# Splitting each K and V load into two column halves issued from two queues, with the slots in memory order

## The chip, the cores and the metric

The kernel runs on one core of one Trainium2 chip. The metric is the device time of one launch in microseconds (us): the kernel before takes 2564.84 us, the median of 3 runs (2564.63 to 2564.92). TensorE is called PE, VectorE DVE, ScalarE ACT, GpSimd POOL and SyncE SP below; a core also has 16 DMA engines, on which every transfer runs.

## What is computed

Two independent attention blocks A and B, each one decode step with a cached K and V, joined at the end:

```python
def _A_ref(x, k_cache, v_cache, wq, wo):
    B, Sq, D = x.shape                 # 8, 1, 1024
    H, Dh = 32, 128
    q = (x @ wq).reshape(B, Sq, H, Dh).transpose(0, 2, 1, 3)
    scores = jnp.einsum("bhqd,bhkd->bhqk", q, k_cache) * (Dh ** -0.5)
    p = softmax(scores)
    o = jnp.einsum("bhqk,bhkd->bhqd", p, v_cache)
    return o.transpose(0, 2, 1, 3).reshape(B, Sq, H * Dh) @ wo
...
return jnp.concatenate([a, b], axis=-1)
```

Everything is bf16. k_cache and v_cache are 8 x 32 x 4096 x 128, that is 268 MB each, and there are four of them; wq and wo are 8.4 MB each. There is one query per batch entry and head, so every byte of K and V is read once and used once.

## The kernel before

**Slots.** The work is cut into 64 slots (NS), 32 for A and 32 for B. A slot n is one batch entry b and one group g of 8 heads. Its K and its V are 8 MB each: 8 heads x 1 MB, which lie next to each other in the cache. `source` (line 292) lays such a block over 128 partitions, 16 partitions to a head, so a partition holds 256 positions of 128 values: one contiguous run of 64 KB. `where` (line 295) gives the order of the slots: b runs fastest, then g, then the block A or B. Consecutive slots are therefore 32 MB apart in the cache.

**Buffers and loads.** kbuf has two buffers of 8 MB (slot n uses n % 2), vbuf one. `load_k` and `load_v` issue one DMA each, all from SP, so all bulk loads stand in one queue in the order of the program. In slot n of the loop (line 497; m = n - 1) the code has load_k(n), then load_v(m), but SP only waits on semaphores and runs ahead of the other engines: as soon as PE has finished the product with V of a slot, vbuf is free, and SP issues the next V and the K two slots on, one behind the other. wq of A and B go through vbuf ahead of the slots. At the end wo of A goes to kbuf buffer 0, the last V (slot 63) to kbuf buffer 1, and wo of B, in five pieces of falling size, again to buffer 0. Pieces of wo are loaded as rows of 64 KB cut in columns: the first piece has runs of 32 KB at a distance of 64 KB.

**One slot of compute.** DVE multiplies K in place by the query, which has been spread over the partitions, in four chunks (`multiply`, L337); PE adds up the 128 values of each position with matmuls against an identity (`add_up`, L347); DVE finishes each chunk (`reduce`, L359) and finds the maximum (`softmax`, L364 to L368). Then PE does the product of slot m's probabilities with V (`pv`, L396), ACT takes the exponentials of slot n (`exps`, L375, eight of them), copies the product out (`copy_o`, L403), and PE gathers it (`gather`, L411) and sums the rows (`rowsum`, L381). Every second slot PE and ACT make the spread query for two slots (`make_qbc`, L325 and L329) from a small copy by POOL (`pick_q`, L318).

**Waits.** A small class Program records what each operation reads and writes by names (k0 and k1 for the two K buffers, v for vbuf) and works out the semaphore waits. PE, ACT and DVE run slots 1 to 62 as a hardware loop of two slots per turn (`rolled`); SP's and POOL's programs are written out. Within a loop nothing but the semaphores' registers changes from turn to turn.

Of the kernel before, what the change touches and what calls it, by code (L numbers as in the profile page):

```python
# [27 lines left out]
class Program:  # L28


    def __init__(self):
        self.order = {e: [] for e in ENGINES}
        self.ops = []
        self.writer = {}
        self.readers = {}
        self.bank = {}
        self.loops = {e: [] for e in ENGINES}

    def add(self, eng, emit, reads=(), writes=(), banks=(), dma=None):
# [104 lines left out]
def _build(nc, caches, out):  # L144
# [23 lines left out]
    with es:  # L168
# [53 lines left out]
        def dma(eng, dst, src, writes, sem, reads=()):  # L222
            return P.add(eng, lambda e: e.dma_start(dst, src), reads=reads, writes=writes, dma=sem)  # L223
# [28 lines left out]
                op.sig = True  # L252

        def load_wq(c):
            dma("sp", vbuf[:], caches[c][3].rearrange("(p r) n -> p (r n)", r=R), ["v"], "v")

        def make_xT(c):
            def emit(e):
# [8 lines left out]
        def make_q(c):  # L267
            w = vbuf[:].rearrange("p (r n) -> p r n", r=R)

            def emit(e):  # L270
                last = None
                for r in range(R):
                    for k in range(8):
                        q = k % 4
                        last = e.matmul(qps[k // 4][0][32 * q:32 * q + B, :], xT[:, c, r, :], w[:, r, k * 512:(k + 1) * 512],  # L275
                                        start=(r == 0), stop=(r == R - 1), tile_position=(0, 32 * q))
                return last
            P.add("pe", emit, reads=["v", "orow"], banks=["oacc", "late"])
            for k in range(2):
                P.add("dve", lambda e, k=k: e.tensor_copy(qrow[k][0], qps[k][0][:]), writes=[qrow[k][1]], banks=[qps[k][1]])  # L280

            def turn(e):
                last = None
                for h in range(H):
                    q, k = (h // 4) % 4, h // 16
                    last = e.matmul(bps[:, h * B:(h + 1) * B], qrow[k][0][:, (h % 4) * Dh:(h % 4 + 1) * Dh],  # L286
                                    ident[:, 32 * q:32 * q + B], start=True, stop=True)
                return last
            P.add("pe", turn, reads=["asb", "osum", "ident"], banks=["bps"])
            P.add("dve", lambda e: e.tensor_copy(qT[:, c, :], bps[:, 0:H * B]), writes=[f"qT{c}"], banks=["bps"])  # L290

        def source(c, what, b, g):
            return caches[c][what][b, g * HP:(g + 1) * HP].rearrange("h (p t) d -> (h p) (t d)", t=T)

        def where(n):
            gi, b = divmod(n, B)
            c, g = divmod(gi, NG)
            return c, g, b

        def load_k(n):  # L300
            c, g, b = where(n)
            dma("sp", kbuf[:, n % 2, :], source(c, 1, b, g), [f"k{n % 2}"], f"k{n % 2}")

        def load_v(m):
            c, g, b = where(m)
            buf, name = (vbuf[:], "v") if m < NS - 1 else (kbuf[:, m % 2, :], f"k{m % 2}")
            dma("sp", buf, source(c, 2, b, g), [name], name)
            vplace[m] = (buf, name)

        def load_wo(c):  # L310
            rows = caches[c][4].rearrange("(p r) n -> p r n", r=RW)
            for j, (lo, hi) in enumerate(pieces[c]):
                dma("sp", wo[:, lo:hi, :], rows[:, lo:hi, :], [f"wo{j}"] if j else ["wo0", "k0"], f"wo{j}")

        def pick_q(n):
            c, g, b = where(n)
            src = qT[:, c, g * HP * B:(g + 1) * HP * B].rearrange("p (h b) -> p b h", b=B)[:, b:b + 2, :]
            P.add("pool", lambda e: e.tensor_copy(qg[:], src.unsqueeze(3).to_broadcast([128, 2, HP, SEG])),  # L318
                  reads=[f"qT{c}"], writes=["qg"])

# [14 lines left out]
        def multiply(n, ch):  # L335
            kv = chunk(n, ch).rearrange("p (t d) -> p t d", d=Dh)
            P.add("dve", lambda e: e.tensor_tensor(  # L337
                kv, kv, qbc[:, n % 2, :].unsqueeze(1).to_broadcast([128, CT, Dh]), ALU.mult),
                reads=[f"k{n % 2}", "qbc"], writes=[f"prod{n % 2}c{ch}"])

        def add_up(n, ch):
            i = ch % 2
            pj = chunk(n, ch).rearrange("p (t j w) -> p t j w", t=CT, w=EW)
            rv = red[i][:].rearrange("p (t w) -> p t w", w=EW)

            def emit(e):
                first = e.matmul(rv, ident[:], pj[:, :, 0, :], start=True, stop=False).ins  # L347
# [6 lines left out]
            P.add("pe", emit, reads=[f"prod{n % 2}c{ch}", f"k{n % 2}", "ident"], banks=[f"red{i}"])  # L354

        def reduce(n, ch):
            i = ch % 2
# [31 lines left out]
        def pv(m):  # L389
            buf, name = vplace[m]  # L390

            def emit(e):
                last = None
                for j in range(CT):
                    q, t = j % 4, j * TB
                    last = e.matmul(oacc[32 * q:32 * q + TB * HP, 0:TB * Dh],  # L396
                                    prob[:, t:t + TB, :].rearrange("p t h -> p (t h)"), buf[:, t * Dh:(t + TB) * Dh],
                                    start=(j < 4), stop=(j >= CT - 4), tile_position=(0, 32 * q))
                return last
            P.add("pe", emit, reads=[name] + probs, banks=["oacc"])  # L400

        def copy_o(m):
            P.add("act", lambda e: e.activation(osb[:], oacc[:], ACTF.Copy), writes=scores, banks=["oacc"])  # L403
# [11 lines left out]
        def heads(m):  # L415
            i = m % 2
            o = 32 + i * HP
            gi, b = divmod(m % NS, B)
# [4 lines left out]
            P.add("dve", lambda e: e.tensor_tensor(on[:, i, :], sps[:, o:o + HP], rl[:, i, :], ALU.mult),  # L423
                  reads=[f"rl{i}"], writes=[f"on{i}"], banks=["sps"])
            P.add("pool", lambda e: e.tensor_copy(ona[:, gi, :, b], on[:, i, :]), reads=[f"on{i}"], writes=[f"ona{gi}"])  # L425
# [28 lines left out]
        def project(c, j):  # L454
            lo, hi = pieces[c][j]

            def emit(e):
                last = None
                for r in range(lo, hi):
                    for q in range(4):  # L460
                        last = e.matmul(acc[32 * q:32 * q + B, 0:CW], onp[:, r, :], wo[:, r, q * CW:(q + 1) * CW],  # L461
                                        start=(r == 0), stop=(r == RW - 1), tile_position=(0, 32 * q))
                return last
            P.add("pe", emit, reads=["onp", f"wo{j}", "k0"], banks=["acc"])

        def write_out(c):
            P.add("dve", lambda e: e.tensor_copy(orow[0:104, :], acc[0:104, 0:CW]), writes=["orow"], banks=["acc"])
# [12 lines left out]
            P.add("pe", emit, reads=["ident"], banks=["red0"])  # L480

        NS = NC * NG * B
        vplace = {}
        pieces = [[(0, RW)], [(0, 16), (16, 24), (24, 28), (28, 30), (30, RW)]]
        load_wq(0)
        load_k(0)
# [9 lines left out]

        for n in range(NS):
            m = n - 1
            if n == NS - 1:
                for e, at in marks().items():  # L500
                    P.loops[e].append((start[e], at, (n - 1) // 2))
            if n == 1:
                start = marks()
            if n >= 1:
                load_k(n)
            if n == NS - 1:
# [33 lines left out]
                pv(m)  # L540
            if n % 2 == 1 and n + 1 < NS:
                make_qbc(n + 1)
            exps(n)
            if m >= 0:
                copy_o(m)
# [43 lines left out]
        def rolled(name, eng, a, b, k):  # L589
            ahead, base, waits = P.rolled(name, a, b, k)  # L590
            for key, val in ahead.items():
                eng.wait_ge(sems[key], val)
            regs = {}
            for key, val in base.items():
                regs[key] = eng.alloc_register(f"w{a}_{key}")
                eng.reg_mov(regs[key], val)
            with eng.Fori(0, k):
                for op, ws in zip(P.order[name][a:], waits):
                    for key, inc in ws:
                        eng.wait_ge(sems[key], regs[key])  # L600
                        eng.reg_add(regs[key], regs[key], inc)  # L601
                    one(name, eng, op)

        def run(name, eng):
            ops, at = P.order[name], 0
# [62 lines left out]
```

## Time and profile before

| | |
|---|---|
| median of 3 runs | 2564.84 us (2564.63 to 2564.92) |
| span of the profiled execution, first to last instruction | 2563.2 us |
| time of the median run that lies around that span | 1.6 us |
| read from HBM | 1107.33 MB, 432 GB/s over the span |
| DVE busy | 1360.0 us, 53% of the span |
| PE busy | 1470.8 us, 57% |
| ACT busy | 652.1 us, 25% |
| mean granted TensorE clock | 0.798 |

The profiled execution's own time is taken as its span and the 1.6 us around it. A row of the timeline gives start, duration, engine, line, operation, written tile <- read tile, the count, and in brackets the idle time ahead of it with what ended it. "SPq" and "ACTq" are the DMA issues of SP and ACT. A row of DMA queues gives packets, MB, and the time that the packets took, as a share of the time of 16 engines in the stretch asked for; a packet counts to the stretch in which it starts, with its whole time, so the share can be over 100%. q1 is SP's queue, q10 ACT's; q8 and q14 fetch instructions.

### The profile page before, as it was taken

Reading aid. Unit: us, or ns where it says so; the run is one execution under the profiler, and the core shown is the slowest. Engines: PE = TensorE matmul, PEld = TensorE weight load, DVE = VectorE, ACT = ScalarE, POOL = GpSimd, SP = SyncE. Lnnn points to the kernel's source line nnn. Section 1 sums busy time; section 2 is a strip of 40 time slices with the busy share of each in tenths; the row PEclk is TensorE's granted clock in tenths of the full one; section 3 lists DMA queues with packets and bytes.
Section 4 is the critical chain, followed back from the end, with each engine's and each line's share of the span. In section 5 each row is a group of like instructions: output and inputs, shape, how many; then the busy total and the mean of one; then the engine's idle time right before and its main releaser. Section 6 shows DMA issues by size and latency. Waiting matters only on the chain.

```text
span 2563.2 us, 19013 instructions
## 1 busy us (share of the span) xinstructions
PE 1470.8 (57%) x9440; PEld 291.3 (11%) x5600; DVE 1360.0 (53%) x913; ACT 652.1 (25%) x1127; POOL 291.1 (11%) x112
## 2 busy tenths in 40 slices
PE   3565565565565565565565565555655655655656
PEld 0101101101101101101011011011011011011012
DVE  3456455455465465465464564564564564554551
ACT  0322322312312313313313313213223223223122
POOL 0111011011011011011011011011011010110110
PEclk8787787787787887887887887877877877878878
DMA  9999999999999999999999999999999999999999
GB/s 425 428 438 430 438 430 437 430 437 431 436 432 436 432 436 432 435 433 435 432 436 432 436 432 436 431 437 431 437 431 437 430 438 430 438 430 438 430 437 386
DMA packets 19755, 1107.52 MB, mean 432 GB/s; under 512 B 2256, under 2 KB 2320, under 8 KB 2592
## 3 DMA queue, kind: packets, MB, share of 16 engines
q1 hardware_dynamic: 19616, 1107.31, 99.9%
q8 instruction: 7, 0.11, 0.0%
q10 hardware_dynamic: 128, 0.06, 0.0%
q14 instruction: 4, 0.03, 0.0%
HBM read 1107.33 MB, written 0.03 MB: 432 GB/s over the span
## 4 chain that ended last, share of the span: by engine, by line
DMA 63%; PE 17%; DVE 14%; issue 6%; SPq 0%; another core or an unknown queue 0%; DVEq 0%
DMA kbuf<-in_B_k_cache_dram 31%; DMA kbuf<-in_A_k_cache_dram 30%; PE red L347 12%; DVE kbuf L337 12%; PE oacc L396 4%; DMA kbuf<-in_B_wo_dram 2%; DVE osb L359 2%; SPq L223 0%; DVE on L423 0%; PE acc L461 0%; DVEq L601 0%; PE oacc L275 0%; PE late L275 0%; PE bps L286 0%
## 5 line engine op out<-in xcount | busy, mean ns | idle before, releaser
L337 DVE TENSOR_TENSOR kbuf<-kbuf,qbc 128x8192 bf16<-128x8192 bf16 x256 | 1128.2, 4408 | 782.9 <-DMA kbuf<-in_A_k_cache_dram 389.8
L347 PE MATMUL red<-kbuf,ident 128*128 128x512 bf16 x4096 | 1050.9, 419 | 392.9 <-DVE kbuf L337 218.7
L375 ACT ACTIVATE prob<-osb,bias 128x256 bf16<-128x256 f32 x512 | 598.7, 1583 | 930.4 <-PE oacc L396 895.6
L425 POOL COPY ona<-on 128x8 bf16<-128x8 bf16 x64 | 278.7, 4354 | 2218.2 <-DVE on L423 2218.2
L411 PE MATMUL sps<-sel,osb 128*128 128x8 f32 x512 | 116.6, 357 | 649.9 <-ACT osb L403 649.7
L359 DVE TENSOR_REDUCE osb<-red 128x64 f32<-128x512 f32 x256 | 176.0, 687 | 305.9 <-PE red L347 305.9
L375 ACT ACTIVATION_READ_ACCUMULATOR prob<-osb,bias 128x1 f32 x512 | 252.9, 494 | 0.0
L329 ACT ACTIVATE qbc<-bps 128x256 bf16<-128x256 f32 x32 | 12.3, 383 | 897.6 <-PE bps L325 897.6
L396 PE MATMUL oacc<-vbuf,prob 128*32 128x512 bf16 x4032 | 231.8, 383 | 10.5 <-DMA vbuf<-in_B_v_cache_dram 10.5
L411 PEld LDWEIGHTS sps<-sel,osb 128*128 128x128 f32 x512 | 112.4, 323 | 669.7 <-issue 667.8
L347 PEld LDWEIGHTS red<-kbuf,ident 128*128 128x128 bf16 x256 | 25.1, 98 | 1191.0 <-issue 1170.3
L396 PEld LDWEIGHTS oacc<-vbuf,prob 128*32 128x32 bf16 x4032 | 102.5, 97 | 324.6 <-issue 219.1
L403 ACT ACTIVATE osb<-oacc 128x512 f32<-128x512 f32 x64 | 38.2, 597 | 15.3 <-PE oacc L396 8.2
L381 PE MATMUL sps<-rsum,ones 128*128 128x8 f32 x128 | 36.6, 360 | 5.4 <-ACT prob L375 5.4
L381 PEld LDWEIGHTS sps<-rsum,ones 128*128 128x128 f32 x128 | 34.7, 331 | 5.5 <-ACT prob L375 5.5
L364 DVE TENSOR_REDUCE rmax<-osb 128x1 f32<-128x256 f32 x64 | 26.9, 420 | 7.6
L423 DVE TENSOR_TENSOR on<-sps,rl 128x8 bf16<-128x8 f32 x64 | 10.1, 158 | 27.9 <-PE sps L381 27.9
L365 DVE STREAM_TRANSPOSE tmax<-rmax 128x32 f32<-128x32 f32 x64 | 13.5, 212 | 7.7
L366 DVE TENSOR_REDUCE nmax<-tmax 128x2 f32<-128x32 f32 x64 | 11.9, 186 | 7.6
L318 POOL COPY qg<-qT 128x256 bf16<-128x256 bf16 x32 | 12.5, 392 | 28.0 <-DVE qT L290 27.4
L368 DVE SCALAR_TENSOR_TENSOR bias<-nmax,neg 128x8 f32<-128x8 f32 x64 | 10.7, 168 | 7.7
L275 PE MATMUL oacc<-vbuf,orow 128*8 128x512 bf16 x64 | 7.7, 472 | 11.4 <-DMA vbuf<-in_A_wq_dram 11.4
(52 smaller groups left out, 104.1 us busy)
## 6 DMA issues: line engine op xcount, KB each, us to landing
kbuf<-in_B_wo_dram SPq DMA_DIRECT2D x1, 4096.0 KB, 39.5
kbuf<-in_B_wo_dram SPq DMA_DIRECT2D x1, 2048.0 KB, 44.0
kbuf<-in_B_wo_dram SPq DMA_DIRECT2D x1, 1024.0 KB, 46.1
kbuf<-in_B_wo_dram SPq DMA_DIRECT2D x2, 512.0 KB, 47.2
kbuf<-in_A_k_cache_dram SPq DMA_DIRECT2D x32, 49.1
vbuf<-in_A_v_cache_dram SPq DMA_DIRECT2D x32, 30.2
kbuf<-in_B_k_cache_dram SPq DMA_DIRECT2D x32, 49.1
vbuf<-in_B_v_cache_dram SPq DMA_DIRECT2D x31, 30.1
```

Of the source, the lines that this page charges most:

```text
L318: P.add("pool", lambda e: e.tensor_copy(qg[:], src.unsqueeze(3).to_broadcast([128, 2, HP, SEG])), reads=[f"qT{c}"], writes=["qg"])
L337: P.add("dve", lambda e: e.tensor_tensor(kv, kv, qbc[:, n % 2, :].unsqueeze(1).to_broadcast([128, CT, Dh]), ALU.mult), reads=[f"k{n % 2}", ...
L347: first = e.matmul(rv, ident[:], pj[:, :, 0, :], start=True, stop=False).ins
L359: P.add("dve", lambda e: e.tensor_reduce(score[:, ch * CT:(ch + 1) * CT], rv, AX.X, ALU.add), writes=[f"score{ch}"], banks=[f"red{i}"])
L364: P.add("dve", lambda e: e.tensor_reduce(rmax[:], score, AX.X, ALU.max), reads=scores, writes=["rmax"])
L365: P.add("dve", lambda e: e.transpose(tmax[:], rmax[:].to_broadcast([128, 32])), reads=["rmax"], writes=["tmax"])
L375: P.add("act", lambda e, h=h: e.activation(prob[:, :, h], score, ACTF.Exp, bias=bias[:, h:h + 1], scale=scale, accum_out=rsum[:, i, h:h + 1]),
L381: P.add("pe", lambda e: e.matmul(sps[:, i * HP:(i + 1) * HP], ones[:].to_broadcast([128, 128]), rsum[:, i, :], start=True, stop=True), rea ...
L396: last = e.matmul(oacc[32 * q:32 * q + TB * HP, 0:TB * Dh], prob[:, t:t + TB, :].rearrange("p t h -> p (t h)"), buf[:, t * Dh:(t + TB) * D ...
L403: P.add("act", lambda e: e.activation(osb[:], oacc[:], ACTF.Copy), writes=scores, banks=["oacc"])
L411: last = e.matmul(sps[:, o:o + HP], osb[:, t * Dh:(t + 1) * Dh], sel[:, t, :], start=(t == 0), stop=(t == TB - 1))
L425: P.add("pool", lambda e: e.tensor_copy(ona[:, gi, :, b], on[:, i, :]), reads=[f"on{i}"], writes=[f"ona{gi}"])
```

## The change

Each K and each V load of a slot becomes two loads. The left one takes the first 32 KB of every partition's 64 KB run, the right one the other 32 KB. The left ones stay on SP; the right ones go to ACT, in `load_right(n)`, which stands behind make_qbc and ahead of exps: there ACT issues the right half of V of slot n and of K of slot n + 2. The first two K and the first V are issued by SP in both halves, and the last V (slot 63) stays one load on SP. The right halves have names and semaphores of their own (k0r, k1r, vr): multiply and add_up of chunks 0 and 1 wait for the left half only, chunks 2 and 3 for the right one; pv waits for both halves of V.

Slots now run through g first and then b, which is the order in which their 8 MB blocks lie in the caches. With that the source of a load in ACT's loop is the loop's counter times two plus a constant. As source A ends and B begins inside the slots, ACT has two loops now, with slots written out between and around them; PE and DVE keep their one loop. pick_q takes two neighbouring groups of heads of one batch entry, where it took two neighbouring batch entries of one group.

```diff
         def where(n):
-            gi, b = divmod(n, B)
-            c, g = divmod(gi, NG)
+            c, r = divmod(n, NG * B)
+            b, g = divmod(r, NG)
             return c, g, b
 
-        def load_k(n):
-            c, g, b = where(n)
-            dma("sp", kbuf[:, n % 2, :], source(c, 1, b, g), [f"k{n % 2}"], f"k{n % 2}")
...
+        def load(n, what, buf, name, right, eng=None):
+            c, r = divmod(n, NG * B)
+            if right is None:
+                P.add("sp", lambda e: e.dma_start(buf, source(c, what, r)), writes=[name, name + "r"], dma=name)
+                return
+            cut = slice(T * Dh // 2, T * Dh) if right else slice(0, T * Dh // 2)
+
+            def emit(e):
+                at = r if P.turn is None else P.turn * 2 + r
+                return e.dma_start(buf[:, cut], source(c, what, at)[:, cut])
+            key = name + "r" if right else name
+            P.add(eng or ("act" if right else "sp"), emit, writes=[key], dma=key)
+
+        def load_k(n, right=False):
+            load(n, 1, kbuf[:, n % 2, :], f"k{n % 2}", right, "sp" if n < 2 else None)
+            if n < 2 and not right:
+                load_k(n, True)
...
+        def load_right(n):
+            if 1 <= n < NS - 1:
+                load_v(n, True)
+            if n + 2 < NS:
+                load_k(n + 2, True)
...
-                reads=[f"k{n % 2}", "qbc"], writes=[f"prod{n % 2}c{ch}"])
+                reads=[f"k{n % 2}" + ("r" if ch >= NCH // 2 else ""), "qbc"], writes=[f"prod{n % 2}c{ch}"])
...
-            P.add("pe", emit, reads=[name] + probs, banks=["oacc"])
+            P.add("pe", emit, reads=[name, name + "r"] + probs, banks=["oacc"])
...
             if n % 2 == 1 and n + 1 < NS:
                 make_qbc(n + 1)
+            load_right(n)
             exps(n)
```

SP, at the start of the program (wq of A, K of slot 0, wq of B, K of slot 1, V of slot 0, K of slot 2, V of slot 1, K of slot 3); before:

```order
L223 DMA vbuf<-in_A_wq_dram 128x32768
L223 DMA kbuf<-in_A_k_cache_dram 128x32768
L223 DMA vbuf<-in_B_wq_dram 128x32768 [waits c_pe,d_v]
L223 DMA kbuf<-in_A_k_cache_dram 128x32768
L223 DMA vbuf<-in_A_v_cache_dram 128x32768 [waits c_pe,d_v]
L223 DMA kbuf<-in_A_k_cache_dram 128x32768
```

and with the change, where x2 is a left and a right half one behind the other:

```order
L224 DMA vbuf<-in_A_wq_dram 128x32768
L310 DMA kbuf<-in_A_k_cache_dram 128x16384 x2
L224 DMA vbuf<-in_B_wq_dram 128x32768 [waits c_pe,d_v]
L310 DMA kbuf<-in_A_k_cache_dram 128x16384 x2
L310 DMA vbuf<-in_A_v_cache_dram 128x16384 [waits c_pe,d_v]
L310 DMA vbuf<-in_A_v_cache_dram 128x16384
L310 DMA kbuf<-in_A_k_cache_dram 128x16384
L310 DMA vbuf<-in_A_v_cache_dram 128x16384 [waits c_pe,d_v]
```

From the K of slot 2 on, SP issues left halves alone, with the waits that it had.

ACT, in its loop, one slot with the spread query and one without; before:

```order
L329 ACTIVATE qbc<-bps 128x256
L601 REGISTER_ALU [waits c_dve]
L375 ACTIVATE prob,rsum<-osb,bias 128x256 x8
L601 REGISTER_ALU [waits c_act]
L403 ACTIVATE osb<-oacc 128x512
L601 REGISTER_ALU [waits c_dve]
L601 REGISTER_ALU [waits c_pe]
```

and with the change (d_vr is the semaphore of the right halves of V; the ISA rows set an address):

```order
L351 ACTIVATE qbc<-bps 128x256
L310 ISA
L310 DMA vbuf<-in_A_v_cache_dram 128x16384
L310 ISA
L310 DMA kbuf<-in_A_k_cache_dram 128x16384
L632 REGISTER_ALU [waits c_dve]
L397 ACTIVATE prob,rsum<-osb,bias 128x256 x8
L632 REGISTER_ALU [waits c_act]
L425 ACTIVATE osb<-oacc 128x512
L632 REGISTER_ALU [waits c_pe]
L632 ISA [waits d_vr]
L310 DMA vbuf<-in_A_v_cache_dram 128x16384
```

The two issues stand ahead of the eight exponentials of each slot, behind the same wait for PE's product with V that held the exponentials before.

DVE, in its loop, between chunk 0 and chunk 3 of a slot; with the change there is one more wait (d_k1r, the right half of K) ahead of chunk 2:

```order
L359 TENSOR_TENSOR kbuf<-kbuf,qbc 128x8192
L632 REGISTER_ALU [waits c_pe]
L381 TENSOR_REDUCE osb<-red 128x64
L632 REGISTER_ALU [waits d_k1r]
L359 TENSOR_TENSOR kbuf<-kbuf,qbc 128x8192
L632 REGISTER_ALU [waits c_pe]
L381 TENSOR_REDUCE osb<-red 128x64
```

Ahead of chunk 0 DVE waits for d_k1 as before, which now stands for the left half.

More of the change, by code (lines that the diff above doesn't have):

```diff
@@ L36, in __init__ @@
         self.bank = {}
+        self.turn = None
         self.loops = {e: [] for e in ENGINES}
@@ L254, in load_wq @@
         def load_wq(c):
-            dma("sp", vbuf[:], caches[c][3].rearrange("(p r) n -> p (r n)", r=R), ["v"], "v")
+            dma("sp", vbuf[:], caches[c][3].rearrange("(p r) n -> p (r n)", r=R), ["v", "vr"], "v")
         def make_xT(c):
@@ L277, in emit @@
                 return last
-            P.add("pe", emit, reads=["v", "orow"], banks=["oacc", "late"])
+            P.add("pe", emit, reads=["v", "vr", "orow"], banks=["oacc", "late"])
             for k in range(2):
@@ L290, in make_q, with source, load_v @@
             P.add("dve", lambda e: e.tensor_copy(qT[:, c, :], bps[:, 0:H * B]), writes=[f"qT{c}"], banks=["bps"])
-        def source(c, what, b, g):
-            return caches[c][what][b, g * HP:(g + 1) * HP].rearrange("h (p t) d -> (h p) (t d)", t=T)
+        def source(c, what, r):
+            return caches[c][what].rearrange("b (g h) (p t) d -> (b g) (h p) (t d)", h=HP, t=T)[r]
         def where(n):
-            gi, b = divmod(n, B)
-            c, g = divmod(gi, NG)
+            c, r = divmod(n, NG * B)
+            b, g = divmod(r, NG)
             return c, g, b
-        def load_k(n):
-            c, g, b = where(n)
-            dma("sp", kbuf[:, n % 2, :], source(c, 1, b, g), [f"k{n % 2}"], f"k{n % 2}")
-        def load_v(m):
-            c, g, b = where(m)
+        def load(n, what, buf, name, right, eng=None):
[13 more added lines that the diff above has]
+                load_k(n, True)
+        def load_v(m, right=False):
             buf, name = (vbuf[:], "v") if m < NS - 1 else (kbuf[:, m % 2, :], f"k{m % 2}")
-            dma("sp", buf, source(c, 2, b, g), [name], name)
+            load(m, 2, buf, name, None if m == NS - 1 else right, None if m else "sp")
+            if m == 0 and not right:
+                load_v(m, True)
             vplace[m] = (buf, name)
+        def load_right(n):
[3 more added lines that the diff above has]
+                load_k(n + 2, True)
         def load_wo(c):
@@ L312, in load_wo @@
             for j, (lo, hi) in enumerate(pieces[c]):
-                dma("sp", wo[:, lo:hi, :], rows[:, lo:hi, :], [f"wo{j}"] if j else ["wo0", "k0"], f"wo{j}")
+                dma("sp", wo[:, lo:hi, :], rows[:, lo:hi, :], [f"wo{j}"] if j else ["wo0", "k0", "k0r"], f"wo{j}")
         def pick_q(n):
             c, g, b = where(n)
-            src = qT[:, c, g * HP * B:(g + 1) * HP * B].rearrange("p (h b) -> p b h", b=B)[:, b:b + 2, :]
+            src = qT[:, c, g * HP * B:(g + 2) * HP * B].rearrange("p (i h b) -> p i h b", i=2, b=B)[:, :, :, b]
             P.add("pool", lambda e: e.tensor_copy(qg[:], src.unsqueeze(3).to_broadcast([128, 2, HP, SEG])),
@@ L353, in emit @@
                 return last
-            P.add("pe", emit, reads=[f"prod{n % 2}c{ch}", f"k{n % 2}", "ident"], banks=[f"red{i}"])
+            P.add("pe", emit, reads=[f"prod{n % 2}c{ch}", f"k{n % 2}" + ("r" if ch >= NCH // 2 else ""), "ident"], banks=[f"red{i}"])
         def reduce(n, ch):
@@ L417, in heads @@
             o = 32 + i * HP
-            gi, b = divmod(m % NS, B)
+            c, g, b = where(m % NS)
+            gi = c * NG + g
             if m == NS - 1:
@@ L463, in emit @@
                 return last
-            P.add("pe", emit, reads=["onp", f"wo{j}", "k0"], banks=["acc"])
+            P.add("pe", emit, reads=["onp", f"wo{j}", "k0", "k0r"], banks=["acc"])
         def write_out(c):
@@ L482, in _build @@
         NS = NC * NG * B
-        vplace = {}
+        NH = NG * B
+        vplace, start = {}, {}
         pieces = [[(0, RW)], [(0, 16), (16, 24), (24, 28), (28, 30), (30, RW)]]
@@ L498, in _build @@
             m = n - 1
[L499 to L503, printed above, removed]
+            if n in (1, NH - 3, NH + 1, NS - 3, NS - 1):
+                now = marks()
+                for e, at in now.items():
+                    if n == NH - 3 or n == NS - 3:
+                        if e == "act":
+                            P.loops[e].append((start[e], at, (n - first) // 2))
+                    elif n == NS - 1 and e != "act":
+                        P.loops[e].append((start[e], at, (n - 1) // 2))
+                    if n == 1 or n == NH + 1 and e == "act":
+                        start[e] = at
+                first = n
             if n >= 1:
@@ L596, in rolled @@
                 eng.reg_mov(regs[key], val)
-            with eng.Fori(0, k):
+            with eng.Fori(0, k) as P.turn:
                 for op, ws in zip(P.order[name][a:], waits):
@@ L602, in rolled @@
                     one(name, eng, op)
+            P.turn = None
         def run(name, eng):
```

## The prediction

> **What bounds the kernel now.** I read the page's slices and DMA lines first, then the chain, then the groups with their idle time, then the timeline of one slot. In the page, the DMA row says how busy the 16 engines are in each 40th of the span:
>
> ```profile
> span 2563.2 us, 19013 instructions
> DMA  9999999999999999999999999999999999999999
> DMA packets 19755, 1107.52 MB, mean 432 GB/s; under 512 B 2256, under 2 KB 2320, under 8 KB 2592
> q1 hardware_dynamic: 19616, 1107.31, 99.9%
> DMA 63%; PE 17%; DVE 14%; issue 6%; SPq 0%; another core or an unknown queue 0%; DVEq 0%
> L337 DVE TENSOR_TENSOR kbuf<-kbuf,qbc 128x8192 bf16<-128x8192 bf16 x256 | 1128.2, 4408 | 782.9 <-DMA kbuf<-in_A_k_cache_dram 389.8
> ```
>
> There is no slice in which the DMA engines rest; q1, SP's queue, has them busy for 99.9% of the span. The chain names PE and DVE for a third, but that is only who released SP's issues; DVE's largest group stands idle for 782.9 us, waiting for K. What counts is whether the queue ever runs dry, and one slot of the timeline answers it:
>
> ```profile
> 1011.25 4.43 DVE L337 TENSOR_TENSOR kbuf<-kbuf,qbc 128x8192 bf16<-128x8192 bf16 x1 [12.94 <-DMA kbuf<-in_A_k_cache_dram]
> ...
> 1035.77 3.63 PE L396 MATMUL oacc<-vbuf,prob 128*32 128x512 bf16 x64
> ...
> 1039.50 0.33 SPq L223 DMA_DIRECT2D vbuf<-in_A_v_cache_dram  x1
> 1039.87 0.43 SPq L223 DMA_DIRECT2D kbuf<-in_A_k_cache_dram  x1
> ...
> 1049.95 4.43 DVE L337 TENSOR_TENSOR kbuf<-kbuf,qbc 128x8192 bf16<-128x8192 bf16 x1 [11.82 <-DMA kbuf<-in_A_k_cache_dram]
> ```
>
> K lands at 1011.25, the slot's compute ends 28.25 us later, SP issues the next two loads at 1039.50, and the K in flight then still needs 10.45 us. So about 10.5 us of transfers are left in the queue at each issue: the kernel is bound by what the engines take per packet, and compute has 10.5 us of slack in each slot.
>
> **The change, part by part.** *The shorter runs.* A load of 8 MB is 128 rows of 64 KB, 8 on each engine. Now each row is two packets. What a packet takes is read from stretches that hold one kind: first 200 to 2400 us, then two stretches within the first piece of B's wo (2539.65 to 2546.80 and 2540.5 to 2546.5), whose rows are 32 KB runs at a distance of 64 KB, the very shape of the new halves.
>
> ```profile
> DMA packets 16365, 953.90 MB, mean 434 GB/s; under 512 B 1808, under 2 KB 1808, under 8 KB 1808
> q1 hardware_dynamic: 16363, 953.88, 100.2%
> ...
> q1 hardware_dynamic: 94, 3.08, 100.0%
> ...
> q1 hardware_dynamic: 79, 2.59, 100.2%
> ```
>
> 953.88 MB / 65,536 B is 14,555 packets of 64 KB; 100.2% of 16 x 2200 us is 35,270 us; less the 1808 small ones (9 ns each, below) that is 2422.1 ns per packet. A packet of 32 KB takes 16 x 7150 x 1.000 / 94 = 1217.0 and 16 x 6000 x 1.002 / 79 = 1217.7, so 1217.4 ns. The share over 100% shows that each record overlaps the next: 70 us over 16,363 records, 4.3 ns each. One packet of 64 KB thus costs 2417.8 ns of engine time, two of 32 KB 2 x 1213.1 = 2426.2: **8.4 ns more**, a gap that each packet brings along. Shares are rounded to 0.1%, which leaves about 1.7 ns either way: 6.7 to 10.1 ns.
>
> 64 loads of K and 63 of V are split: 127 x 8 = 1016 more packets on each engine, 1016 x 8.4 ns = **8.5 us** (6.8 to 10.3).
>
> *The second semaphore.* Each load ends with a 4-byte packet on each engine; one of them, alone in 10 ns from 640.825 us:
>
> ```profile
> q1 hardware_dynamic: 1, 0.00, 5.6%
> ```
>
> 5.6% of 160 ns is 9 ns, less the overlap 4.7; 127 more per engine are **0.6 us**.
>
> *Two queues on the same engines.* The only place where SP's and ACT's queues carry data together is the start, where x lies in rows of 2 KB in ACT's queue between SP's 64 KB packets (7.23 to 7.70 us):
>
> ```profile
> q1 hardware_dynamic: 14, 0.92, 450.3%
> q10 hardware_dynamic: 8, 0.02, 8.9%
> ```
>
> A q10 packet takes 83.7 ns there, and the q1 packets of the stretch 4.503 x 7520 / 14 = 2418.8 ns, so no longer than elsewhere: changing queues costs nothing visible, and it hides nothing either, since the second 32 KB of a long packet take 2422.1 - 1217.4 = 1204.7 ns, by which rate 2 KB are 75.3 ns, and 83.7 less the overlap leaves a gap of 4.1 ns. I take 0 for it, from this row. The bounds below are the rivals.
>
> The Trainium skill says in "DMA: Bandwidth & Descriptors", "Issuing engines are not separate DMA queues", that DMAs started by different engines run on the same 16 engines and interleave, and that starting them on several saves only the issue time. By that the sum has no term for the second queue, which agrees with these rows; its being small depends on eight packets.
>
> *ACT's two issues per slot.* They stand ahead of the exponentials. Its issues at the start took 0.59 and 0.29 us, so I estimate 0.6 to 1.2 us per slot.
>
> ```profile
> 0.74 0.59 ACTq L223 DMA_DIRECT2D prob<-in_A_x_dram  x1
> 1.37 0.29 ACTq L223 DMA_DIRECT2D prob<-in_B_x_dram  x1
> ...
> 1049.48 0.60 ACT L403 ACTIVATE osb<-oacc 128x512 f32<-128x512 f32 x1
> ...
> 1051.90 0.57 PE L381 MATMUL sps<-rsum,ones 128*128 128x8 f32 x2
> 1054.51 9.09 PE L347 MATMUL red<-kbuf,ident 128*128 128x512 bf16 x32 [2.03 <-DVE on L423]
> ```
>
> Behind the issues wait exps, the copy (L403), gather and rowsum, and behind these PE's first add_up (L347). PE stands idle there for 2.03 us, which covers them; were it not so, the slack in the queue does. 0 us.
>
> *The order in the two queues.* If the engines take packets from both queues in turn, a slot's right halves pass what SP has queued. At the start before:
>
> ```profile
> 43.61 8.76 DVE L337 TENSOR_TENSOR kbuf<-kbuf,qbc 128x8192 bf16<-128x8192 bf16 x2 [11.93 <-DMA kbuf<-in_A_k_cache_dram]
> ...
> 70.84 0.33 SPq L223 DMA_DIRECT2D vbuf<-in_A_v_cache_dram  x1
> ...
> 82.40 4.43 DVE L337 TENSOR_TENSOR kbuf<-kbuf,qbc 128x8192 bf16<-128x8192 bf16 x1 [8.83 <-DMA kbuf<-in_A_k_cache_dram]
> ```
>
> A load of 8 MB is 19.4 us (8 x 2.42), a half 9.7. Slot 0 starts on its left half 9.7 us earlier, at about 34, and frees its buffer near 57 (four chunks took 24.5 us above, from 1011.25 to 1035.77; two remain when the right half lands at 43.6). ACT then puts K of slot 2, right half, into an empty queue; it shares the engines with wq of B until 69 and with K of slot 1, whose left half lands at 82.4 as now, its right half at 92, V of slot 0 at 111.5, K of slot 2 at 121.2. PE's product with V waits for that V, ends near 115.1, and the next loads are issued at about 115.3 with 5.9 us left in SP's queue, none in ACT's. From there: with M us left in SP's queue at an issue, served at half speed, K lands 2M later; compute takes 28 us more; the engines have 38.7 us of new work. So M becomes 38.7 + M - 2M - 28 = 10.7 - M: 5.9, 4.8, 5.9 and so on. The queues never run dry; half of the slack is gone, at no cost. The 9.7 us gained at the start buy nothing, as the engines were already busy.
>
> *Memory order.* Each load still reads one block of 8 MB in rows of 64 KB distance; only the distance between blocks shrinks. Nothing in the rows depends on it: 0.
>
> *The end.* The last packet of wo is used at 2559.66 (row below), and all ends 3.5 us later; the change moves nothing there. At the last issue of V halves 38.8 + M us of work are queued (wo of A 19.4, two halves of V); K of slot 63 lands after 2M and frees the buffer for the last V 24.5 us on, at 36 for M = 5.9, 8 us before the engines could rest. More of ACT's program is written out, which may add one or two instruction fetches of 16 KB; one such packet at 34.39 us took 6.100 x 160 = 976 ns on one engine, so 0 to 3 us; I take 0, as it delays one engine of 16.
>
> ```profile
> q8 instruction: 1, 0.02, 610.0%
> ...
> 2559.66 0.39 PE L461 MATMUL acc<-kbuf,onp 128*8 128x256 bf16 x8 [0.81 <-DMA kbuf<-in_B_wo_dram]
> ```
>
> **Sum:** 8.5 + 0.6 = 9.1 us on the span of 2563.2, so 2572.3; with the 1.6 us around it, as for the median of 2564.84, **2573.9 us**, 0.35% slower. Its own range is 6.8 + 0.6 to 10.3 + 0.6 + 3: 2572 to 2579.
>
> **The rivals.** *(a) The second queue hides the gap.* While one queue's packet ends, the other's might already flow. If no gap is left, each 32 KB costs the 1204.7 ns by which the longer packet exceeds the shorter one: 1016 x (2417.8 - 2 x 1204.7) = -8.5 us, with the semaphores -7.9, **2556.9 us**, faster. It pays from the point where the gap per packet is under half of 8.4 ns, 4.2, since there are twice as many. For it: nothing yet ran with both queues full. Against it: the 2 KB packets between SP's kept a gap. *(b) Half the gap.* That same 4.1 ns behind a change of queue may hold for long packets too: then the doubled count is paid and only the semaphores are left, **2565.4 us**, no change. The Trainium skill, in "DMA: Bandwidth & Descriptors", "Why small descriptors are slow (HBM only)", gives a fixed overhead of about 3 cycles per packet; with the 850 MHz of "Where 436 GB/s comes from" that is, as an estimate, 3.5 ns and a sum of 3.6 + 0.6 us, inside this case too; the 8.4 ns speak against it. *(c) Changing queues stalls the engine.* Behind an instruction packet of another queue one SP packet took 17.338 x 160 = 2774 ns (the row of 10 ns at 639.36 us):
>
> ```profile
> q1 hardware_dynamic: 1, 0.07, 1733.8%
> ```
>
> That is 352 ns more than 2422. At 2032 changes it is 715 us, 3280 us. The q10 row speaks against it: behind eight changes there was nothing. *(d) The queues run dry,* since ACT's issues or the late half of V cost more than 10.7 us in two slots. Each us beyond it is paid in each of 31 pairs: 2 us beyond give 62 us, 2627.
>
> **How the numbers follow.** 0.2% (5.1 us) is about what a measurement of this kernel tells from no change. Forecast 0.55; (a) 0.18, faster; (b) 0.20, the same; (c) and (d) 0.07 together, slower. So faster 0.18, same 0.20, slower 0.62. The range takes in the forecast, (b), and (a) to its end, and leaves out (c), (d) and a gap somewhat larger than any row shows: 2556.5 to 2580.
>
> **What would show it.** In the new profile: q1 and q10 share the bytes about evenly, some 32,500 packets of 32 KB; right halves of V land about 19 us after their issue and left ones about 30; the time of 16 engines divided by the packets of a stretch gives 1213 ns per 32 KB (1204.7 for (a), 1209 for (b)); DVE still waits for K in each slot, with half of the slack. I am wrong if the DMA row has slices below 9 (d), or if that quotient is not 1213.

## The result and the profile after

The changed kernel takes **2576.32 us** (median of 4 runs, 2575.96 to 2577.2) against 2564.84 us before (2564.63 to 2564.92): 11.5 us more, a ratio of 1.0045 with the interval [1.0033, 1.0057]. The profiled run took 2576.45 us, 2573.9 of them in its span, which is 10.7 us longer than the span before.

The page of the changed kernel: span, the 16 DMA engines in 40 slices, packets, the two queues (packets, MB, share), the chain, and DVE's largest group (busy, mean ns, idle and what ended it).

```profile
span 2573.9 us, 19455 instructions
...
DMA  9999999999999999999999999999999999999998
...
DMA packets 38045, 1107.54 MB, mean 430 GB/s; under 512 B 4288, under 2 KB 4352, under 8 KB 4624
...
q1 hardware_dynamic: 20048, 587.22, 53.0%
q10 hardware_dynamic: 17984, 520.16, 47.0%
...
DMA 55%; PE 19%; DVE 15%; issue 6%; another core or an unknown queue 3%; ACT 2%; SPq 0%; DVEq 0%; ACTq 0%
...
L359 DVE TENSOR_TENSOR kbuf<-kbuf,qbc 128x8192 bf16<-128x8192 bf16 x256 | 1128.3, 4408 | 770.4 <-DMA kbuf<-in_B_k_cache_dram 373.8
```

The bytes are the same, the packets nearly twice as many (38,045 for 19,755), and the engines are still busy in every slice but the last: nothing waits that did not wait before. The same engines simply take longer for the same bytes. How much per packet is read from the stretch of 200 to 2400 us, as for the kernel before:

```profile
DMA  9999999999999999999999999999999999999999
...
DMA packets 32606, 949.89 MB, mean 432 GB/s; under 512 B 3616, under 2 KB 3616, under 8 KB 3616
...
q10 hardware_dynamic: 16301, 474.91, 50.2%
q1 hardware_dynamic: 16302, 474.95, 50.2%
```

The two queues share the bytes evenly. 100.4% of 16 x 2200 us is 35,341 us; less the 3616 small packets at 9 ns, divided by the other 28,987 packets, it is 1218.1 ns per 32 KB. The 0.4% (141 us) over 32,603 records is an overlap of 4.3 ns each, so a packet takes 1213.8 ns net, where 1213.1 was forecast and (a) would have shown 1204.7, (b) 1209.

The timeline of one slot in the middle of the changed kernel (start, duration, what ran, idle time before it in brackets):

```profile
1004.46 0.33 SPq L310 DMA_DIRECT2D vbuf<-in_A_v_cache_dram  x1
1004.74 0.37 ACTq L310 DMA_DIRECT2D vbuf<-in_A_v_cache_dram  x1
1004.83 0.43 SPq L310 DMA_DIRECT2D kbuf<-in_A_k_cache_dram  x1
...
1005.28 0.34 ACTq L310 DMA_DIRECT2D kbuf<-in_A_k_cache_dram  x1
...
1014.94 4.43 DVE L359 TENSOR_TENSOR kbuf<-kbuf,qbc 128x8192 bf16<-128x8192 bf16 x1 [11.85 <-DMA kbuf<-in_A_k_cache_dram]
1015.23 0.60 ACT L425 ACTIVATE osb<-oacc 128x512 f32<-128x512 f32 x1
...
1019.50 9.13 PE L369 MATMUL red<-kbuf,ident 128*128 128x512 bf16 x32 [1.27 <-DVE on L446]
...
1042.66 0.33 SPq L310 DMA_DIRECT2D vbuf<-in_A_v_cache_dram  x1
```

At the issue at 1004.46 the K in flight still needs 10.48 us, as much as before (10.45): the slack of compute has not shrunk. ACT's two issues take 0.37 and 0.34 us, and PE's rest ahead of add_up, which was to cover them, is 1.27 us, down from 2.03.

### The profile page after: what moved, and what is told of

Same layout as the page of the kernel before. It is cut to its first block, busy times and chain, and to the rows that moved or that the text cites. A ratio compares the mean times of both kernels' runs of the same rounds, so it can differ in the third digit from the quotient of the medians.

```text
span 2573.9 us, 19455 instructions
## 1 busy us (share of the span) xinstructions
PE 1480.3 (58%) x9440; PEld 293.3 (11%) x5600; DVE 1360.6 (53%) x913; ACT 655.9 (25%) x1127; POOL 291.2 (11%) x112
## 2 busy tenths in 40 slices
DMA packets 38045, 1107.54 MB, mean 430 GB/s; under 512 B 4288, under 2 KB 4352, under 8 KB 4624
## 4 chain that ended last, share of the span: by engine, by line
DMA 55%; PE 19%; DVE 15%; issue 6%; another core or an unknown queue 3%; ACT 2%; SPq 0%; DVEq 0%; ACTq 0%
DMA kbuf<-in_B_k_cache_dram 29%; DMA kbuf<-in_A_k_cache_dram 19%; DVE kbuf L359 13%; PE red L369 13%; PE oacc L418 5%; DMA kbuf<-in_A_wo_dram 2%; DMA vbuf<-in_A_v_cache_dram 2%; DMA kbuf<-in_B_wo_dram 2%; ACT prob L397 1%; DMA vbuf<-in_B_wq_dram 1%; DVE osb L381 1%; DMA vbuf<-in_A_wq_dram 1%; SPq L310 0%; PE sps L433 0%
## 5 line engine op out<-in xcount | busy, mean ns | idle before, releaser
L484 PE MATMUL acc<-kbuf,onp 128*8 128x256 bf16 x256 | 11.9, 357 | 6.1 <-DMA kbuf<-in_A_wo_dram 4.7
## 6 DMA issues: line engine op xcount, KB each, us to landing
vbuf<-in_A_v_cache_dram SPq DMA_DIRECT2D x33, 4096.0 KB, 30.3
vbuf<-in_A_v_cache_dram ACTq DMA_DIRECT2D x31, 4096.0 KB, 31.1
vbuf<-in_B_v_cache_dram ACTq DMA_DIRECT2D x31, 4096.0 KB, 31.1
```

## The experiments

Runs 1 to 4 were on one chip, runs 5 to 8 on another; the kernel before, run beside them, took 2564.91 us on the first and 2565.0 us on the second. My theory: each packet brings a gap of some 9 ns, whatever queue it comes from, and the 1016 more packets per engine are the loss. The rivals: the second queue costs it (both queues on one engine, ACT's issues, or the queues running dry), or the order of the slots in memory does.

**1. Both halves from SP.** The changed kernel without the second queue:

```diff
-        def load_k(n, right=False):
-            load(n, 1, kbuf[:, n % 2, :], f"k{n % 2}", right, "sp" if n < 2 else None)
...
+        def load_k(n):
+            for right in (False, True):
+                load(n, 1, kbuf[:, n % 2, :], f"k{n % 2}", right, "sp")
...
-            load_right(n)
```

> Both halves of every load are issued by SP, so runs of 32 KB, twice the semaphores and the memory order stay, and the second queue goes. Theory of the gap (each packet costs about 9 ns beside its bytes, whichever queue it is in): 1016 more packets and 127 more semaphore packets per engine, 9.9 us over the kernel before, about 2575 us. Rival, the second queue or ACT's issues cost the time: back to about 2565 us. If the queue costs only what the gap leaves open of the 11.5 us measured, 1 to 2 us under the changed kernel.

Measured: 2574.30 us (2574.14 to 2574.49), ratio 1.0036 [1.0023, 1.005], 9.4 us more than before. From 200 to 2400 us its one queue stands so:

```profile
q1 hardware_dynamic: 32604, 949.89, 100.3%
```

The gap theory holds: of the 11.5 us, 9.4 are there without a second queue. Less 0.6 us for the semaphores (their records take 1.27 us per engine before and 2.41 us here, and 4.3 ns of each of the 127 new ones is overlap) it is 8.8 us, **8.7 ns per added packet**. The rest, 2.0 us here and 1.3 by run 6, comes with the second queue.

**2. Whole loads, two queues.** V(n) and K(n + 2) of odd n are issued by ACT, those of even n by SP, in runs of 64 KB:

```diff
...
+        def load_k(n):
+            if n < 3 or n % 2 == 0:
+                load(n, 1, kbuf[:, n % 2, :], f"k{n % 2}")
...
         def load_right(n):
-            if 1 <= n < NS - 1:
-                load_v(n, True)
-            if n + 2 < NS:
-                load_k(n + 2, True)
+            if n % 2 == 1 and n < NS - 1:
+                load(n, 2, vbuf[:], "v", "act")
+                load(n + 2, 1, kbuf[:, 1, :], "k1", "act")
```

> Loads are whole again (runs of 64 KB, one semaphore each), in memory order, but V of each odd slot and the K two slots on are issued by ACT, those of even slots by SP, so both queues carry data at once for most of the time. Theory of the gap: as many packets as before, about 2565 us, at most 1 us more. Rival, two queues on the same engines cost the time: about 2575 us.

Measured: 2573.52 us, but spread from 2566.7 to 2575.57; ratio 1.0034 [1.0021, 1.0048]. Both theories missed: neither the gap nor a fixed price of a second queue gives 9 us that come and go. The profile is of the run with 2566.7 us. Its packets took no longer (200 to 2400 us: 100.2% for 14,545 packets of 64 KB and 1811 small ones, 2424 ns each, against 2422 before):

```profile
q10 hardware_dynamic: 8289, 483.46, 50.8%
q1 hardware_dynamic: 8067, 469.77, 49.4%
```

but what is left in the queues at an issue swings from slot to slot. Its timeline, a narrow slot and then two neighbours:

```profile
853.79 0.33 SPq L305 DMA_DIRECT2D vbuf<-in_A_v_cache_dram  x1
...
856.74 4.42 DVE L350 TENSOR_TENSOR kbuf<-kbuf,qbc 128x8192 bf16<-128x8192 bf16 x1 [4.32 <-DMA kbuf<-in_A_k_cache_dram]
...
1007.85 0.33 SPq L305 DMA_DIRECT2D vbuf<-in_A_v_cache_dram  x1
...
1011.73 4.43 DVE L350 TENSOR_TENSOR kbuf<-kbuf,qbc 128x8192 bf16<-128x8192 bf16 x1 [5.25 <-DMA kbuf<-in_A_k_cache_dram]
...
1043.14 0.34 ACTq L305 DMA_DIRECT2D vbuf<-in_A_v_cache_dram  x1
...
1055.27 4.43 DVE L350 TENSOR_TENSOR kbuf<-kbuf,qbc 128x8192 bf16<-128x8192 bf16 x1 [13.89 <-DMA kbuf<-in_A_k_cache_dram]
```

K comes 3.9 us after the issue of the next loads, then 12.1, and at 853.79 only 3.0. That is a swing as I had forecast it for the changed kernel, but not with the numbers of that formula: 3.9 and 12.1 add up to 16, where M and 10.7 - M make 10.7, and the next two slots have 8.5 and 12.4. So a new theory for this run: where the swing goes to its narrow side, the queues run dry in some executions. Run 8 tries it.

The trace shows one more thing that can narrow a slot. The issue of a K, 0.43 us in the kernel before, takes 2.2 to 5.2 us in 43 slots of this run, on either engine. Where it is ACT's, the exponentials stand behind it. This is the slot ahead of the narrow one at 853.79:

```profile
813.53 4.12 ACTq L305 DMA_DIRECT2D kbuf<-in_A_k_cache_dram  x1
817.77 1.43 ACT L388 ACTIVATE prob<-osb,bias 128x256 bf16<-128x256 f32 x1 [4.52 <-issue]
```

Each of the eight slots with 4.0 us or less follows such an issue by ACT, of 4 to 5 us. Why the issues take so long is open.

**3. The memory order alone.** The kernel before, with its loads whole and on SP, and only the order of the slots changed:

```diff
-            gi, b = divmod(n, B)
-            c, g = divmod(gi, NG)
+            c, r = divmod(n, NG * B)
+            b, g = divmod(r, NG)
...
```

> The kernel before with only the order of the slots changed (groups of heads first, then batch entries). Theory of the gap: no change, 2565 us within 1 us. Rival, the order in the caches matters for the reads: a time off 2565 by several us to either side; if the order gave a gain that the shorter runs hide, under 2563 us.

Measured: 2564.84 us (2564.66 to 2565.55, 11 runs), ratio 1.0 [0.9991, 1.0009]. The order costs and gains nothing that this shows (the interval is 0.1% to either side, some 2.3 us); as the cause of the 11.5 us it falls.

**4 and 5. Shorter runs still.** Left and right take turns within a row, by 16 KB (two packets of each per row) and by 4 KB (eight of each):

```diff
-            cut = slice(T * Dh // 2, T * Dh) if right else slice(0, T * Dh // 2)
+            def cut(t):
+                return t.rearrange("p (a s w) -> p a s w", s=2, w=T * Dh // 4)[:, :, 1 if right else 0, :]
```

(w=2048 in the second; multiply and add_up wait for the halves accordingly.)

> As the changed kernel, with as many loads, semaphores and queues, but the left load takes quarters 0 and 2 of each row and the right one quarters 1 and 3: runs of 16 KB, 2032 more packets per engine than the changed kernel. Theory of the gap: 2032 x 9.1 ns = 18.5 us more than the changed kernel's 2576.3, about 2595 us. Rival, the loss hangs on the number of loads, the semaphores or the second queue: no change from 2576 us.

Measured: 2593.60 us (2593.52 to 2594.09), ratio 1.0112 [1.0097, 1.0128]. That is 17.3 us over the changed kernel for 127 x 16 = 2032 more packets per engine, **8.5 ns each**. The slices show that the time is no rest; from 200 to 2400 us:

```profile
DMA  9999999999999999999999999999999999999999
...
DMA packets 61120, 942.63 MB, mean 428 GB/s; under 512 B 3586, under 2 KB 3586, under 8 KB 3586
...
q1 hardware_dynamic: 30557, 471.26, 50.3%
q10 hardware_dynamic: 30560, 471.34, 50.3%
```

> As the changed kernel, with as many loads, semaphores and queues, but left and right loads take every other 4 KB of each row: 16 packets where the changed kernel has 2, 14,224 more per engine. Theory of the gap, if each packet of 4 KB brings the 9.1 ns of a longer one: 129 us more, about 2706 us. If the gap of a short packet is the one that the last pieces of wo show (160.4 ns less 4.3 of overlap less 150.6 at the full rate: 5.5 ns): 16 x 156.1 - 2 x 1213.6 = 70 ns per 64 KB, 72 us more, about 2648 us. Rival, the loss hangs on loads, semaphores or queues: about 2576 us.

Measured: 2724.91 us (2722.41 to 2725.4, one at 2759.11), ratio 1.0664 [1.0607, 1.0722]: 131.3 us over run 4 for 127 x 96 = 12,192 more packets per engine, 10.8 ns each. The expectation with 9.1 ns was 19 us short, that with 5.5 ns 77. The engines do not rest here either, in the same stretch:

```profile
DMA  9999999999999999999999999999999999999999
...
DMA packets 223401, 901.05 MB, mean 410 GB/s; under 512 B 3424, under 2 KB 3424, under 8 KB 223398
```

But the 10.8 ns are not all gap. By the MB of the three stretches (949.86, 942.60 and 901.02 in 16 x 2200 us), 64 KB take an engine 2428.6 ns in the changed kernel, 2447.3 in run 4 and 2560.3 here: 18.7 ns for 2 more packets and 113.0 ns for 12 more, **9.4 ns each** both times. At that price the 12,192 packets make 114.6 us; the other 17 us are paid outside the stretch. Near the end the engines rest for some 7 us; from 2660 to 2680 us, in slices of 0.5 us:

```profile
DMA  9999999999999999977642100000000000990000
```

At the start SP's issues take long, and the packets with them: 183.8 ns each from 70 to 120 us, 164.0 from 200 to 2400, which is some 5 us per engine. Where the last 4 or 5 us go is not traced.

```profile
72.97 21.95 SPq L311 DMA_DIRECT2D vbuf<-in_A_v_cache_dram  x2
```

So the gap comes with every added packet, 8.7 to 9.4 ns, from 64 KB down to 4 KB. What no run parts is the packet from the jump: each added packet also starts a run that does not adjoin the one before it.

**6. The changed kernel again,** unchanged, beside the runs that follow.

> The changed kernel as it is, so that it stands on the same chip as the run with all halves on ACT. 2576 us if the 2.0 us by which it exceeded the run with both halves on SP belong to it; about 2574.5 us if they were the chip's.

Measured: 2575.58 us (2574.67 to 2576.54), ratio 1.0039 [1.0026, 1.0053]: 10.6 us more than before, and 1.3 us more than run 1. The second queue's share is small. The 95% intervals of the two ratios overlap, so its size (1.3 and 2.0) is not sharp; but all nine executions of the changed kernel (2574.67 to 2577.2) lie above all five of run 1 (2574.49 at most).

**7. Both halves from ACT,** from V of slot 1 and K of slot 2 on. If it is ACT's issues that cost, they are doubled here; if it is having two queues, it goes away in the middle of the kernel:

```diff
...
         def load_right(n):
-            if 1 <= n < NS - 1:
-                load_v(n, True)
-            if n + 2 < NS:
-                load_k(n + 2, True)
+            for right in (False, True) if 1 <= n < NS - 1 else ():
+                load(n, 2, vbuf[:], "v", right, "act")
+            for right in (False, True) if n + 2 < NS else ():
+                load(n + 2, 1, kbuf[:, n % 2, :], f"k{n % 2}", right, "act")
```

> From slot 1's V and slot 2's K on, both halves of every load are issued by ACT, four issues per slot ahead of the exponentials, and SP's queue carries only the start and the end. Runs, semaphores and order as in the changed kernel. If the 2 us above the run with both halves on SP come from sharing the engines between two queues: about 2574.5 us. If they come from ACT's issues, which delay the exponentials: 2576 us or more, up to 2578 us. Theory of the gap for the rest: not under 2574 us.

Measured: 2585.28 us (2584.9 to 2585.7), ratio 1.0078 [1.0064, 1.0092]. Both expectations missed, by 7 to 11 us, and one place pays nearly all of it. Its DMA engines from 110 to 140 us, in slices of 0.75 us:

```profile
DMA  9699795996912000000000009909699199791993
```

and the timeline around it:

```profile
48.49 10.55 ACTq L310 DMA_DIRECT2D kbuf<-in_A_k_cache_dram  x2
...
121.03 6.06 PE L416 MATMUL oacc<-vbuf,prob 128*32 128x512 bf16 x64 [6.32 <-DMA vbuf<-in_A_v_cache_dram]
...
127.59 0.87 ACTq L310 DMA_DIRECT2D vbuf<-in_A_v_cache_dram  x2
128.63 0.92 ACTq L310 DMA_DIRECT2D kbuf<-in_A_k_cache_dram  x2
```

Both halves of K of slot 2 are issued by ACT from 48.49 us on, and share the engines with wq of B and V of slot 0 in SP's queue. V, which is needed first, lands last, at 121, together with everything else; the next loads wait for PE's product with it, until 127.59, and in between the engines rest. That is rival (d), once. In the middle of the kernel ACT's queue alone does what SP's did in run 1:

```profile
q10 hardware_dynamic: 32605, 949.93, 100.3%
```

so ACT's issues of halves, four in each slot, cost nothing there: that part of the rival falls. (The long issues of run 2 are another matter.)

**8. Run 2 with more slack:** chunk 3 isn't multiplied, which gives compute 4.4 us more in each slot.

```diff
         def multiply(n, ch):
+            if ch == NCH - 1:
+                return
```

> The run with whole loads issued by SP and ACT in turn, with chunk 3's multiplication by the query left out (its scores are sums of K alone), which shortens the compute of a slot by about 5 us and so adds 5 us of slack to each pair of margins (10.7 to about 16 us per two slots); bytes, packets and queues are the same. If that run lost its 6 to 9 us because the queues ran dry where a slot's margin was under 4 us: 2566 us, all runs within 1 us. If two queues with runs of 64 KB cost the time themselves: 2572 to 2576 us again.

Measured: 2566.66 us (2565.65 to 2568.28, 11 runs), ratio 1.0007 [0.9998, 1.0016]. With the slack the 9 us are gone, and most of the spread (2.6 us for 8.9), though the issues of K are as long here as in run 2 (up to 5.2 us). This points to want of slack in run 2, not to packets. That its queues ran dry is argued from it, not shown: no profile caught run 2 in one of its long executions, and run 8 was on the other chip. Nor does this run leave the second queue a large price of its own: 1.7 us, the size of the remainder in runs 1 and 6.

## Why the prediction was right, and where not

The forecast was 2573.9 us, 9.1 more than before; it came to 11.5, in the same direction and for the reason given. By its own steps:

- **The shorter runs** (8.5 us, 6.8 to 10.3): 8.8 by run 1. The gap read from two stretches of the trace before, 8.4 ns, is 8.7 (run 1), 8.5 (run 4) and 9.4 (the middle of runs 4 and 5). The Trainium skill, in "DMA: Bandwidth & Descriptors", "Why small descriptors are slow (HBM only)", has about 3 cycles per packet, as an estimate 3.5 ns; the measured 8.5 to 9.4 ns decide against it.
- **The second semaphore** (0.6 us): 0.6 by its records. No run takes it away by itself.
- **Two queues on the same engines** (0): the mis-sized term, 1.3 to 2.0 us. (a) and (b) fall, since the gap stays whole with the queues in turn, and so does (c): at 2032 changes there are not 715 us. (The sum in (a) has its terms the wrong way round; it is 2 x 1204.7 - 2417.8 that makes 8.5 us less.) In the middle the second queue costs nothing that shows: run 1 and the changed kernel both move 949.9 MB from 200 to 2400 us. Where the time shows is the end. The landing times of the last piece of wo, on the first and on the last of the 16 engines, worked out from the trace of each:

| | first engine, us | last engine, us | apart, us |
|---|---|---|---|
| before | 2557.34 | 2559.61 | 2.27 |
| both halves from SP (1) | 2567.04 | 2569.35 | 2.31 |
| changed | 2567.13 | 2570.70 | 3.57 |
| changed again (6) | 2567.69 | 2571.20 | 3.51 |

In run 1 the engines end as far apart as before; in the changed kernel the last ends 1.35 us later than in run 1 (1.85 in run 6), the first 0.1 us (0.65). The product with wo must wait for the last. The timeline of PE's last product with wo, of the changed kernel:

```profile
2570.74 0.39 PE L484 MATMUL acc<-kbuf,onp 128*8 128x256 bf16 x8 [0.36 <-DMA kbuf<-in_B_wo_dram]
```

and of run 1:

```profile
2569.39 0.39 PE L476 MATMUL acc<-kbuf,onp 128*8 128x256 bf16 x8 [0.61 <-DMA kbuf<-in_B_wo_dram]
```

Of these 1.35 us 1.2 are left in the spans (2573.9 and 2572.7). With the time around the span, 2.55 us in the profiled execution where I had taken 1.6, this makes up most of what was missing. Why an engine falls behind is open. The landings of one load lie 1.7 us apart up to 121 us and 2.8 us at 140, so it begins about where ACT's queue starts for good. But a second queue alone does not bring it: worked out the same way, the last landings are 2.32 us apart in run 4, 2.08 in run 5, 1.95 in run 2 and 2.40 in run 8, all with two queues. Nor do fetches of instructions, which the prediction gave 0 to 3 us: the pages of run 1 and of the changed kernel count as many of them (7 packets in q8, 6 in q14).
- **ACT's two issues** (0): right. They took 0.76 us of PE's 2.03 us of rest (1.27 are left), and run 7 doubles them without loss in the middle of the kernel.
- **The order in the two queues**: no cost, as forecast, but **the step to "half of the slack is gone" failed**. The margin in the middle is 10.5 us, and V's halves land together, 30.3 and 31.1 us after the issue (19 and 30 forecast), K's too; the page's rows of DMA issues:

```profile
vbuf<-in_A_v_cache_dram SPq DMA_DIRECT2D x33, 4096.0 KB, 30.3
kbuf<-in_B_k_cache_dram SPq DMA_DIRECT2D x32, 4096.0 KB, 49.4
kbuf<-in_B_k_cache_dram ACTq DMA_DIRECT2D x32, 4096.0 KB, 50.1
vbuf<-in_A_v_cache_dram ACTq DMA_DIRECT2D x31, 4096.0 KB, 31.1
```

The start went nearly as drawn (slot 0 from 33.98, K of slot 1 at 82.17, V of slot 0 at 111.36). The next issue came at 117.24 where 115.3 was forecast, and DVE starts on K of slot 2 at 121.08, so the margin was 3.8 us, not 5.9:

```profile
33.98 8.76 DVE L359 TENSOR_TENSOR kbuf<-kbuf,qbc 128x8192 bf16<-128x8192 bf16 x2 [2.67 <-ACT qbc L351]
...
58.65 0.36 ACTq L310 DMA_DIRECT2D kbuf<-in_A_k_cache_dram  x1
...
82.17 4.43 DVE L359 TENSOR_TENSOR kbuf<-kbuf,qbc 128x8192 bf16<-128x8192 bf16 x1 [10.46 <-DMA kbuf<-in_A_k_cache_dram]
...
111.36 5.79 PE L418 MATMUL oacc<-vbuf,prob 128*32 128x512 bf16 x64 [4.67 <-DMA vbuf<-in_A_v_cache_dram]
...
117.24 0.33 SPq L310 DMA_DIRECT2D vbuf<-in_A_v_cache_dram  x1
117.67 0.37 ACTq L310 DMA_DIRECT2D vbuf<-in_A_v_cache_dram  x1
...
121.08 4.42 DVE L359 TENSOR_TENSOR kbuf<-kbuf,qbc 128x8192 bf16<-128x8192 bf16 x1 [11.85 <-DMA kbuf<-in_A_k_cache_dram]
```

But I let ACT's queue share the engines at once. From its issue at 117.67 to 121.2 there are SP's packets alone:

```profile
q1 hardware_dynamic: 60, 1.44, 98.0%
```

Only then, from 121.2 to 122.2, come ACT's:

```profile
q10 hardware_dynamic: 15, 0.49, 114.4%
```

By then SP's old work is done, both queues hold the same, and each slot adds the same to both: they stay even, and the margin grows back to 10.5 us (5.2, 6.6, 7.9, 9.3 and 10.6 in the next five slots). Where only one queue gets work in a slot (run 2) the margin swings, but not by the formula either. *(d)* did not happen in the changed kernel; run 7 pays it once, and run 2, as argued above, in most executions. How near the changed kernel came to it is not shown: its margin was 3.8 us, once, and run 2's profiled execution had 3.0 and lost nothing that shows.
- **Memory order** (0): right, run 3. **The end** (0 to 3 us, 0 taken): the rest behind the last product is 3.2 us (3.5 before); no term.

## What to carry to other kernels

Where the DMA engines never rest, count the packets per engine and charge each its gap, some 9 ns here, even on runs of 32 KB: it can be read from a stretch of the old trace that holds the new shape of packet. A second issuing queue adds no rate to engines that are full; it does add an order between queues that the program no longer fixes, so follow the first slots by hand and look at the margin where an empty queue gets its first work. Look also at how long the issues take (4 to 5 us in run 2) on an engine that has work of its own behind them. Of these versions none beats the kernel before.

## What the hardware showed beside this

- The gap hardly depends on the size of the packet: 8.7 ns between 64 and 32 KB (run 1), and in the middle of the kernel 9.4 between 32 and 16 KB (run 4) and 9.4 between 16 and 4 KB (run 5).
- The issue of a whole K of 64 KB runs took 0.43 us with one queue (before) and up to 5.2 us with two queues in turn (run 2).
- A queue that was empty is served late while another is full: 3.5 us after the issue in the rows above, and as much at the start (issue at 58.65, first packet of q10 at 62.13, with SP's queue full). In run 7, on engines at rest, the first packets came 0.9 to 1.1 us after it (none from 127.59 to 128.5, five by 128.7). The Trainium skill, in "DMA: Bandwidth & Descriptors", "Latency and other measured facts", has about 600 ns to the first byte and up to 2 us of memory latency at high load; where the engines rest the trace shows about 1.0 us from the start of the issue and 0.65 from its end, near the first of these; with a full queue beside it, it cannot part latency from two packets of SP's (2.4 us) that still went first.
- In the changed kernel the 16 engines end 3.5 us apart, in run 1 2.3 (table above). Two queues with shorter runs (runs 4 and 5) end 2.1 to 2.3 us apart, so it is not the second queue by itself.
